# A DiT attention block: V with its features on the partitions, V Wo gated first, and the probabilities applied last

## The chip, the cores and the metric

The kernel runs on one core of one Trainium2 chip. The core has a matrix engine (TensorE, PE in the profile), a vector engine (VectorE, DVE), an activation engine (ScalarE, ACT), a general engine (GpSimd, POOL), and a sequencer that issues transfers (SyncE, SP). The metric is the device time of one execution in microseconds. It was 95.58 us before the change, the median of three runs (95.51 to 95.72). The profile was taken from one further execution, of 95.64 us.

## The reference: what is computed

```python
B, N, D = (2, 256, 1152)
mod = (_silu(c) @ w_mod).reshape(B, 6, 1, D)
shift_a, scale_a, gate_a, shift_m, scale_m, gate_m = [mod[:, i] for i in range(6)]
h = _layernorm(x, axis=-1) * (1 + scale_a) + shift_a
qkv = h @ wqkv
q, k, v = (qkv[..., :D].copy(), qkv[..., D:2 * D].copy(), qkv[..., 2 * D:].copy())
p = _softmax(jnp.einsum('bqd,bkd->bqk', q, k) * D ** (-0.5), axis=-1)
a = jnp.einsum('bqk,bkd->bqd', p, v) @ wo
return x + gate_a * a
```

All inputs and the output are bfloat16. There is one head of 1152 features. The last two lines are what the change regroups: x + gate * ((P V) Wo) can be computed as x + P ((V Wo) * gate), because the gate depends on the batch and the output column and not on the token.

## The kernel before, in words

The 512 tokens are four blocks of 128 (`TT`), two to a batch (`NQ`); the 1152 features are nine blocks of 128 (`KT`) or three chunks of 384 (`CW`, `NCH`). The program order of each engine is the order in the source: the helpers `ten`, `vec`, `sca`, `gps` and `spq` record every instruction, and `pin` at the end fixes that order, so every engine's instructions show the recorder's line, 85, and the profile is read by tile names. PSUM is eight banks, given out in turn by `bank` from a ring, so a sum's bank is taken again eight sums later.

Up to the scores nothing is changed. `hT` is the modulated h with features on the partitions, `qkT` holds q and k in the same way, `s_tiles` are the scores. The softmax (`scores`, `exps`, `probs`) runs on VectorE and ScalarE beside TensorE, and `turn` transposes the probabilities by DMA into `pT_sbs` (keys on the partitions). The gate takes another way: VectorE sums w_mod times silu(c) into `gacc` (`gate_steps`), and GpSimd adds over the partitions with two `partition_all_reduce`, one for each batch, into `gate_bc`, which then holds the gate on every partition. GpSimd starts them only after the last of VectorE's gate steps (`gate_done`).

The part that the change replaces has three stages on TensorE:

- Lines 622 to 628 and 648 (`v_group`): V with the tokens on the partitions, 12 groups (four token blocks by three column chunks) of nine matmuls of 384 columns. ScalarE copies each group to `v_sb`.
- Lines 663 to 672: for each batch, P V transposed, two feature blocks to a bank, 36 matmuls of 256 columns. VectorE and ScalarE copy them in turn to `attnT`.
- Lines 674 to 711: attnT times Wo, block of tokens by block. A sum is multiplied by the gate into `ga` (VectorE), x is added to it (VectorE), and a block is stored by SP when its row is whole. The last block of tokens goes in column chunks of 448, 288, 224 and 192 with stores of their own.

For the last chunk of the last block the gate is multiplied into 192 columns of Wo ahead of time (`wo_last`, by `gated_columns`): eight of nine feature blocks by VectorE between its sums, the ninth by GpSimd behind its second all-reduce. There x enters the sum as one more matmul (identity times x), ScalarE copies the sum out, and the store is issued on ScalarE's own DMA queue.

SP's DMA queue carries all loads, in the order of need (V's weights in three column chunks `chunks_w`, then Wo in three), then the four transposes, then the stores.

Of the kernel before, what the change touches and what calls it, by code (L numbers as in the profile page):

```python
# [8 lines left out]
ALU = mybir.AluOpType  # L9
AX = mybir.AxisListType  # L10
F32 = mybir.dt.float32
BF16 = mybir.dt.bfloat16
# [4 lines left out]
def kernel(  # L17
# [9 lines left out]
    nc = tc.nc  # L27
    P = 128
    B, N, D = x.shape
    T = B * N  # L30
    KT = D // P
    TT = T // P
    NQ = N // P
    CW = 384
    NCH = D // CW
# [10 lines left out]
    out_f = out.rearrange("b n d -> (b n) d")  # L46
# [7 lines left out]
    act = ctx.enter_context(tc.tile_pool(name="act", bufs=1))  # L54
    work = ctx.enter_context(tc.tile_pool(name="work", bufs=2))
    const = ctx.enter_context(tc.tile_pool(name="const", bufs=1))
# [9 lines left out]
    def bank(shape, name, dtype=None, where=None):  # L66
        if where is None:
            where = ring[turn_no[0] % len(ring)]
            turn_no[0] += 1
        return where[0].tile(shape, dtype or F32, tag=where[1], name=name)  # L70
# [21 lines left out]
    vec = _Rec(nc.vector, dve_seq)  # L92
    sca = _Rec(nc.scalar, act_seq)
    ten = _Rec(nc.tensor, pe_seq)
    spq = _Rec(nc.sync, sp_seq)
# [14 lines left out]
    def one(t):  # L110
        return slice(t * P, (t + 1) * P)
# [3 lines left out]
    ident = const.tile([P, P], BF16)  # L115
    gps.memset(ident, 0.0)
    gps.affine_select(
        out=ident, in_=ident, compare_op=ALU.not_equal, fill=1.0, base=0,
# [8 lines left out]
        out=mask, in_=mask, compare_op=ALU.is_ge, fill=0.0, base=0,  # L127
# [3 lines left out]
        out=mask, in_=mask, compare_op=ALU.is_ge, fill=0.0, base=2,  # L131
# [4 lines left out]
    x_sb = act.tile([P, TT, D], BF16)  # L136
# [7 lines left out]
    chunks_w = [wpool.tile([P, KT, CW], BF16, tag=f"wchunk{i}", name="wV") for i in range(NCH)]  # L144
# [121 lines left out]
    hT = act.tile([P, KT, T], BF16)  # L266
# [69 lines left out]
    def evac(on_dve, out_ap, in_ap):  # L336
        if on_dve:
            return vec.tensor_copy(out=out_ap, in_=in_ap)
        return sca.copy(out=out_ap, in_=in_ap)
# [201 lines left out]
    wO = wmpool.tile([P, KT, D], BF16, tag="wH")  # L541
# [31 lines left out]
    for f in range(QACC, KT):  # L573
        ps = bank([P, T], "psQ")
# [6 lines left out]
    for b in range(B):  # L581
        s_ps = bank([P, NQ, N], "s_ps")
        for i in range(NQ):
            tq = b * NQ + i
            for k in range(KT):
                ten.matmul(s_ps[:, i, :], lhsT=qkT[:, k, tq * P : (tq + 1) * P], rhs=qkT[:, KT + k, tok(b)],
                           start=(k == 0), stop=(k == KT - 1))
        s_tiles.append(s_ps)

    nmxs, p_fs, rsums, pns, pT_sbs = {}, {}, {}, {}, []  # L590
# [26 lines left out]
            spq.dma_start_transpose(out=pT[:, :, i * P : (i + 1) * P], in_=pns[b][:, i, :])  # L617
        pT_sbs.append(pT)

    v_sb = act.tile([P, TT, D], BF16, tag="a1")  # L620

    def v_group(gidx):
        t, vc = divmod(gidx, NCH)
        wt = chunks_w[vc]
        ps = bank([P, CW], "ps")
        for k in range(KT):
            ten.matmul(ps, lhsT=hT[:, k, t * P : (t + 1) * P], rhs=wt[:, k, :], start=(k == 0), stop=(k == KT - 1))
        evac(False, v_sb[:, t, vc * CW : (vc + 1) * CW], ps)

    gate_bc = act.tile([P, B, D], F32, tag="gb")  # L630

    gate_steps(11)
# [12 lines left out]
        ar = gps.partition_all_reduce(gate_bc[:, b, :], gacc[:, b, :], P, bass.bass_isa.ReduceOp.add)  # L645
        tc.add_manual_dep(ar.ins, gate_done, SYNC_SCHED, reason="keep gpsimd off the shared port")

    for gidx in range(TT * NCH):
        v_group(gidx)

    attnT = act.tile([P, KT, T], BF16, tag="a2")
    TAIL = (192,)
    TAILW = sum(TAIL)
    wo_last = const.tile([P, KT, TAILW], BF16)

    def gated_columns(eng, k0, k1):
        eng.tensor_tensor(out=wo_last[:, k0:k1, :], in0=wO[:, k0:k1, D - TAILW :],
                          in1=gate_bc[:, B - 1, D - TAILW :].unsqueeze(1).to_broadcast([P, k1 - k0, TAILW]),
                          op=ALU.mult)

    gated_columns(gps, KT - 1, KT)

    for b in range(B):
        for gi, dv0 in enumerate(range(0, KT, 2)):
            ndv = min(2, KT - dv0)
            ps = bank([P, 2, N], "ps")
            for dd in range(ndv):
                dv = dv0 + dd
                for j in range(NQ):
                    ten.matmul(ps[:, dd, :], lhsT=v_sb[:, b * NQ + j, dv * P : (dv + 1) * P],  # L670
                               rhs=pT_sbs[b][:, j, :], start=(j == 0), stop=(j == NQ - 1))
            evac(gi % 2 == 0, attnT[:, dv0 : dv0 + ndv, b * N : (b + 1) * N], ps[:, :ndv, :])

    todo = {4: (0, 3), 6: (3, 6), 8: (6, KT - 1)}
    for t in range(TT):
        b = t // NQ
        o_sb = work.tile([P, D], BF16, tag="o_sb")
        if t < TT - 1:
            chunks = [(oc * CW, CW) for oc in range(NCH)]
            dma_after = {NCH - 1: (0, D)}  # L680
        else:
            chunks, c0 = [], 0
            for w_ in (448, 288, 224) + TAIL:
                chunks.append((c0, w_))
                c0 += w_
            dma_after = {1: (0, chunks[2][0]), 2: (chunks[2][0], D - TAILW), 3: (D - TAILW, D)}
        for ci, (c0, w_) in enumerate(chunks):
            cs = slice(c0, c0 + w_)
            last = (t == TT - 1) and (ci == len(chunks) - 1)
            pregated = (t == TT - 1) and c0 >= D - TAILW  # L690
            ps = bank([P, w_], "ps")
            if pregated:
                ten.matmul(ps, lhsT=ident, rhs=x_sb[:, t, cs], start=True, stop=False)
            for k in range(KT):
                ten.matmul(
                    ps, lhsT=attnT[:, k, t * P : (t + 1) * P],
                    rhs=(wo_last[:, k, c0 - (D - TAILW) : c0 - (D - TAILW) + w_] if pregated else wO[:, k, cs]),
                    start=(k == 0 and not pregated), stop=(k == KT - 1),
                )
            if pregated:  # L700
                sca.copy(out=o_sb[:, cs], in_=ps)
            else:
                ga = work.tile([P, 448], F32, tag="ga")
                vec.tensor_tensor(out=ga[:, :w_], in0=ps, in1=gate_bc[:, b, cs], op=ALU.mult)
                vec.tensor_tensor(out=o_sb[:, cs], in0=ga[:, :w_], in1=x_sb[:, t, cs], op=ALU.add)
                if t * NCH + ci in todo:
                    gated_columns(vec, *todo[t * NCH + ci])
            if ci in dma_after:
                d0, d1 = dma_after[ci]
                dma_eng = nc.scalar if last else spq  # L710
                dma_eng.dma_start(out=out_f[t * P : (t + 1) * P, d0:d1], in_=o_sb[:, d0:d1])

    pin(pe_seq)
    pin(dve_seq)
# [33 lines left out]
```

## Time and profile before

| | us |
|---|---|
| median of three runs | 95.58 |
| the profiled execution | 95.64 |
| its span, first to last instruction | 93.9 |
| TensorE busy | 88.6 |
| VectorE busy | 70.3 |
| ScalarE busy | 34.0 |
| GpSimd busy | 21.2 |
| V, from its first matmul to that of the next stage | 51.76 to 69.31 |
| P V | 69.31 to 73.24 |
| attnT times Wo, its last matmul's end | 73.24 to 91.07 |

The page gives busy times for each engine. A matmul's record is longer than its share of TensorE, since matmuls are pipelined: a group's pace is read from the starts of the stages. A row of a timeline has the start, the length, the engine, the line, the operation, what it writes and reads, its shape and the number of merged instructions; in brackets stands how long the engine was idle before it and what ended that. `ps` are the sums in PSUM, and all three stages above use that name. A row of the chain of waits has the start, the length and the engine with the line. In the list of transfers the last number of a row is the time from issue to landing.

### The profile page before, as it was taken

How to read it: one execution, taken by the hardware profiler on the slowest of the kernel's cores; microseconds unless marked ns; L12 is line 12 of the kernel's file. 1: busy time of each engine (PE TensorE's matmuls, PEld its weight loads, DVE VectorE, ACT ScalarE, POOL GpSimd, SP SyncE). 2: the span in 40 equal slices, each digit the busy share in tenths (PEclk: the TensorE clock that was granted, in tenths of full speed). 3: DMA queues.
4: the chain of work that ended last, by engine and by line, in shares of the span. 5: the costliest groups of instructions: out<-in, count | busy, mean ns of one | idle time of the engine just before them, and what ended most of it. 6: DMA issues, size and time to landing. Idle time of an engine off the chain costs nothing.

```text
span 93.9 us, 1692 instructions
## 1 busy us (share of the span) xinstructions
PE 88.6 (94%) x664; PEld 52.9 (56%) x664; DVE 70.3 (75%) x134; ACT 34.0 (36%) x69; POOL 21.2 (23%) x26
## 2 busy tenths in 40 slices
PE   3989899999999999999999999999999999999980
PEld 1358684545445444444469656565679656655660
DVE  2498689254997988999998899990018587899980
ACT  5189689002553610284320688324246300000010
POOL 5623000810000000000000000008999990003000
PEclk9999999999999999999999999999999999999999
DMA  2999999999999999999999602200000000303123
GB/s 29 334 309 377 380 392 358 377 411 409 405 406 410 409 410 412 399 373 366 383 409 411 269 9 56 61 2 0 0 0 0 0 0 7 126 0 126 57 92 103
DMA packets 17232, 21.31 MB, mean 227 GB/s; under 512 B 2377, under 2 KB 10569, under 8 KB 17225
## 3 DMA queue, kind: packets, MB, share of 16 engines
q1 hardware_dynamic: 16809, 21.15, 62.1%
q8 instruction: 5, 0.08, 0.4%
q10 hardware_dynamic: 416, 0.05, 0.4%
q14 instruction: 2, 0.02, 0.0%
HBM read 19.76 MB, written 1.18 MB: 223 GB/s over the span
## 4 chain that ended last, share of the span: by engine, by line
PE 86%; DMA 6%; SPq 4%; issue 1%; ACT 0%
PE ps L85 42%; PE psQ L85 19%; PE acc L85 10%; PE psK L85 7%; DMA wK<-in_wqkv_dram 6%; PE s_ps L85 4%; SPq L85 4%; PE psE L85 2%; PE psS L85 1%; PE psH L85 1%; PE tp L85 1%; ACT o_sb L85 0%; PE bc_ps L85 0%; PE pT L85 0%
## 5 line engine op out<-in xcount | busy, mean ns | idle before, releaser
L85 POOL PARTITION_ALL_REDUCE gate_bc<-gacc x2 | 13.7, 6886 | 44.6 <-DVE gacc L85 44.6
L85 DVE SCALAR_TENSOR_TENSOR gacc<-wG,scT_f,gacc 128x1152 f32<-128x1152 bf16 x16 | 22.4, 1416 | 0.4
L85 PE MATMUL ps<-wV,hT 128*128 128x384 bf16 x108 | 17.7, 326 | 0.0
L85 PE MATMUL psQ<-hT,wQ 128*128 128x512 bf16 x81 | 17.6, 379 | 0.0
L85 PE MATMUL ps<-wO,attnT 128*128 128x384 bf16 (+3 forms) x108 | 17.0, 319 | 0.0
L85 PEld LDWEIGHTS <-attnT 128*128 128x128 bf16 x117 | 11.3, 98 | 6.3
L85 PEld LDWEIGHTS <-hT 128*128 128x128 bf16 x108 | 10.6, 98 | 6.9
L85 PEld LDWEIGHTS <-wK 128*128 128x128 bf16 x109 | 9.4, 97 | 7.5 <-DMA wK<-in_wqkv_dram 0.7
L85 PEld LDWEIGHTS <-wQ 128*128 128x128 bf16 x81 | 7.9, 98 | 9.5
L85 PE MATMUL acc<-hTs,wK 128*128 128x512 bf16 (+2 forms) x65 | 11.2, 313 | 0.0
L85 ACT CAST qkT<-psQ 128x512 bf16<-128x512 f32 x9 | 4.9, 597 | 10.6 <-PE psQ L85 10.6
L85 DVE CAST attnT<-ps 128x512 bf16<-128x512 f32 (+1 forms) x6 | 3.5, 603 | 6.8 <-PE ps L85 6.8
L85 ACT CAST v_sb<-ps 128x384 bf16<-128x384 f32 x12 | 5.5, 476 | 7.9 <-PE ps L85 7.9
L85 DVE TENSOR_TENSOR ga<-ps,gate_bc 128x384 f32<-128x384 f32 (+3 forms) x12 | 6.4, 537 | 2.3 <-PE ps L85 2.3
L85 PE MATMUL psK<-hTs,wK 128*128 128x512 bf16 x28 | 7.0, 379 | 0.0
L85 DVE TENSOR_TENSOR o_sb<-ga,x_sb 128x384 bf16<-128x384 f32 (+3 forms) x12 | 6.5, 542 | 0.4
L85 ACT CAST o_sb<-ps 128x192 bf16<-128x192 f32 x1 | 0.3, 318 | 17.3 <-PE ps L85 17.3
L85 DVE TENSOR_TENSOR hT<-hTs,held 128x512 bf16<-128x512 bf16 x9 | 5.7, 682 | 0.4 <-ACT held L85 0.4
L85 PE MATMUL junk_ps<-junk 128*128 128x512 bf16 x11 | 4.1, 553 | 1.5 <-DVE junk L85 1.5
L85 DVE BATCH_NORM_STATS2 stats<-x_sb 128x6 f32<-128x384 bf16 x6 | 3.1, 542 | 2.2 <-DMA x_sb<-in_x_dram 2.2
L85 PE MATMUL ps<-pT,v_sb 128*128 128x256 bf16 x36 | 4.1, 272 | 0.0
L85 PE MATMUL s_ps<-qkT 128*128 128x256 bf16 x36 | 4.1, 273 | 0.0
(81 smaller groups left out, 83.2 us busy)
## 6 DMA issues: line engine op xcount, KB each, us to landing
wG<-in_w_mod_dram SPq DMA_DIRECT2D x3, 864.0 KB, 12.5
wV<-in_wqkv_dram SPq DMA_DIRECT2D x3, 864.0 KB, 13.4
wO<-in_wo_dram SPq DMA_DIRECT2D x3, 864.0 KB, 9.1
wH<-in_w_mod_dram SPq DMA_DIRECT2D x2, 1152.0 KB, 9.5
wQ<-in_wqkv_dram SPq DMA_DIRECT2D x4, 576.0 KB, 11.7
wK<-in_wqkv_dram SPq DMA_DIRECT2D x7, 288.0 KB, 7.3
wS<-in_w_mod_dram SPq DMA_DIRECT2D x3, 320.0 KB, 5.9
x_sb<-in_x_dram SPq DMA_DIRECT2D x3, 288.0 KB, 3.2
```

The lines of the kernel that those rows point to most:

```text
L85: r = fn(*a, **k)
```

## The change

V is now computed with its features on the partitions (`vT`): nine groups of nine matmuls of 512 columns, copied by ScalarE. Then u = (V Wo) * gate with the tokens on the partitions (`vo`): VectorE multiplies by the gate as it takes a sum out of PSUM, so u is complete but for P. Then P u (`attend`), two matmuls for each token block and column chunk, with the transposed probabilities as weights; VectorE adds x on the way out into `o_sb`, which is now one tile for all four blocks. `ga` and `attnT` are gone.

The two stages are interleaved by hand, so that P on a chunk comes one or two `vo` groups after the `vo` groups that it reads. The column chunks are 384 wide in batch 0; in batch 1 the last chunk is split into 256 (`CL`) and 128 (`CE`). The last 128 columns use Wo with the gate of batch 1 already in it (`wo_last`, now 128 wide and used for both blocks of batch 1), so ScalarE can copy these sums to u. For the last piece of block 3 x enters by the identity matmul and ScalarE copies and stores, as before; the other pieces end on VectorE and SP. In the last steps the two halves of P u on `CE` are split, so that the first halves of blocks 2 and 3 come ahead of the second halves. There are seven stores where there were six.

```diff
-    for gidx in range(TT * NCH):
-        v_group(gidx)
...
+    vT = act.tile([P, KT, T], BF16, tag="a1")
+    for f in range(KT):
+        wt, i = chunks_w[f // NCH], f % NCH
+        ps = bank([P, T], "psV")
+        for k in range(KT):
+            ten.matmul(ps, lhsT=wt[:, k, i * P : (i + 1) * P], rhs=hT[:, k, :], start=(k == 0), stop=(k == KT - 1))
+        evac(False, vT[:, f, :], ps)
...
+    u_sb = act.tile([P, TT, D], BF16, tag="a2")
+    o_sb = act.tile([P, TT, D], BF16, name="o_sb")
+    wo_last = const.tile([P, KT, P], BF16)
...
     gated_columns(gps, KT - 1, KT)
...
+    def vo(t, c0, w_):
+        cs = slice(c0, c0 + w_)
+        ps = bank([P, w_], "psU")
+        for f in range(KT):
+            ten.matmul(ps, lhsT=vT[:, f, one(t)], rhs=wO[:, f, cs] if w_ > P else wo_last[:, f, :],
+                       start=(f == 0), stop=(f == KT - 1))
+        if w_ > P:
+            vec.tensor_tensor(out=u_sb[:, t, cs], in0=ps, in1=gate_bc[:, t // NQ, cs], op=ALU.mult)
         else:
+            sca.copy(out=u_sb[:, t, cs], in_=ps)
...
+    def attend(t, c0, w_, steps=range(NQ), on_act=False):
+        b, i = divmod(t, NQ)
+        cs = slice(c0, c0 + w_)
+        for j in steps:
+            if j == 0:
+                pso[t] = bank([P, w_], "psO")
+                if on_act:
+                    ten.matmul(pso[t], lhsT=ident, rhs=x_sb[:, t, cs], start=True, stop=False)
+            ten.matmul(pso[t], lhsT=pT_sbs[b][:, j, i * P : (i + 1) * P], rhs=u_sb[:, b * NQ + j, cs],
+                       start=(j == 0 and not on_act), stop=(j == NQ - 1))
+        if NQ - 1 not in steps:
+            return
+        if on_act:
+            sca.copy(out=o_sb[:, t, cs], in_=pso[t])
+        else:
+            vec.tensor_tensor(out=o_sb[:, t, cs], in0=pso[t], in1=x_sb[:, t, cs], op=ALU.add)
+
+    CA, CB, CC = [(i * CW, CW) for i in range(NCH)]
+    CL, CE = (2 * CW, CW - P), (D - P, P)
+    vo(0, *CA)
+    vo(1, *CA)
+    vo(0, *CB)
+    attend(0, *CA)
+    vo(1, *CB)
+    attend(1, *CA)
+    vo(0, *CC)
+    attend(0, *CB)
+    vo(1, *CC)
+    attend(1, *CB)
+    vo(2, *CA)
+    attend(0, *CC)
+    store(0, 0, D)
+    gated_columns(vec, 0, 3)
+    vo(3, *CA)
+    attend(1, *CC)
+    store(1, 0, D)
+    gated_columns(vec, 3, 6)
+    vo(2, *CB)
+    attend(2, *CA)
+    gated_columns(vec, 6, KT - 1)
+    vo(3, *CB)
+    attend(3, *CA)
+    vo(2, *CL)
+    attend(2, *CB)
+    vo(3, *CL)
+    attend(3, *CB)
+    store(3, 0, CL[0])
+    vo(2, *CE)
+    attend(2, *CL)
+    store(2, 0, CE[0])
+    vo(3, *CE)
+    attend(3, *CL)
+    store(3, CL[0], CE[0])
+    attend(2, *CE, steps=range(1))
+    attend(3, *CE, steps=range(1), on_act=True)
+    attend(2, *CE, steps=range(1, NQ))
+    attend(3, *CE, steps=range(1, NQ), on_act=True)
+    store(2, CE[0], D)
+    store(3, CE[0], D, sca)
```

More of the change, by code (lines that the diff above doesn't have):

```diff
@@ L618, in turn @@
         pT_sbs.append(pT)
[L620 to L628, printed above, removed]
     gate_bc = act.tile([P, B, D], F32, tag="gb")
@@ L646 @@
         tc.add_manual_dep(ar.ins, gate_done, SYNC_SCHED, reason="keep gpsimd off the shared port")
-    for gidx in range(TT * NCH):
-        v_group(gidx)
[L651 to L654, printed above, removed]
+    vT = act.tile([P, KT, T], BF16, tag="a1")
[5 more added lines that the diff above has]
+        evac(False, vT[:, f, :], ps)
@@ L656, in gated_columns @@
+    u_sb = act.tile([P, TT, D], BF16, tag="a2")
+    o_sb = act.tile([P, TT, D], BF16, name="o_sb")
+    wo_last = const.tile([P, KT, P], BF16)
     def gated_columns(eng, k0, k1):
-        eng.tensor_tensor(out=wo_last[:, k0:k1, :], in0=wO[:, k0:k1, D - TAILW :],
-                          in1=gate_bc[:, B - 1, D - TAILW :].unsqueeze(1).to_broadcast([P, k1 - k0, TAILW]),
-                          op=ALU.mult)
+        eng.tensor_tensor(out=wo_last[:, k0:k1, :], in0=wO[:, k0:k1, D - P :],
+                          in1=gate_bc[:, B - 1, D - P :].unsqueeze(1).to_broadcast([P, k1 - k0, P]), op=ALU.mult)
@@ L661 @@
     gated_columns(gps, KT - 1, KT)
[L663 to L680, printed above, removed]
-        else:
[L682 to L711, printed above, removed]
@@ new lines, in vo, with store @@
+    def vo(t, c0, w_):
[6 more added lines that the diff above has]
+            vec.tensor_tensor(out=u_sb[:, t, cs], in0=ps, in1=gate_bc[:, t // NQ, cs], op=ALU.mult)
+        else:
+            sca.copy(out=u_sb[:, t, cs], in_=ps)
+    def store(t, c0, c1, eng=spq):
+        eng.dma_start(out=out_f[t * P : (t + 1) * P, c0:c1], in_=o_sb[:, t, c0:c1])
@@ new lines @@
+    pso = {}
+    def attend(t, c0, w_, steps=range(NQ), on_act=False):
[14 more added lines that the diff above has]
+            vec.tensor_tensor(out=o_sb[:, t, cs], in0=pso[t], in1=x_sb[:, t, cs], op=ALU.add)
```

## The prediction

> **What bounds the kernel now.** I read the span and the engine lines first, then the chain of waits, then the timeline of each engine from 50 us to the end. The span:
>
> ```profile
> span 93.9 us, 1692 instructions
> PE 88.6 (94%) x664; PEld 52.9 (56%) x664; DVE 70.3 (75%) x134; ACT 34.0 (36%) x69; POOL 21.2 (23%) x26
> PEclk9999999999999999999999999999999999999999
> ```
>
> TensorE is busy to the end, at full granted clock in every slice. The chain of waits (start, length, what) says whether anything else counts; the early rows price small matmuls:
>
> ```profile
> 1.19 0.06 issue
> ...
> 10.78 0.82 PE acc L85 x10
> ...
> 12.32 0.32 PE acc L85 x5
> ...
> 30.51 17.48 PE psQ L85 x81
> 48.00 3.93 PE s_ps L85 x36
> 51.93 39.15 PE ps L85 x262
> 91.08 0.02 issue
> 91.10 0.32 ACT o_sb L85
> ```
>
> From 30.51 to 91.08 the chain is TensorE alone. So the change is worth what it does to the number and width of matmuls, to waits between them, and to what follows the last one. The starts of the stages, from TensorE's timeline (start, length):
>
> ```profile
> 51.76 17.71 PE L85 MATMUL ps<-wV,hT 128*128 128x384 bf16 x108
> 69.31 4.09 PE L85 MATMUL ps<-pT,v_sb 128*128 128x256 bf16 x36
> 73.24 16.99 PE L85 MATMUL ps<-wO,attnT 128*128 128x384 bf16 x108
> 90.07 0.25 PE L85 MATMUL ps<-x_sb,ident 128*128 128x192 bf16 x1
> 90.16 0.91 PE L85 MATMUL ps<-wo_last,attnT 128*128 128x192 bf16 x9
> ```
>
> 108 V matmuls of 384 columns fill 69.31 - 51.76 = 17.55 us: 0.1625 us each, with no wait. The 36 of 256 columns take 73.24 - 69.31 = 3.93: 0.109 each. 81 of 512 take 17.48 (psQ): 0.216 each. The ten acc pieces at 10.78 are five of 256 and five of 128 columns: (0.82 - 5 x 0.109) / 5 = 0.055 us for 128 columns. The pitch is columns over 2.4 per ns plus 2.5 ns; the 27 matmuls of 448, 288 and 224 columns inside the 73.24 row fit it too.
>
> **The change on TensorE.** V becomes V^T: 81 matmuls of 512 columns in place of 108 of 384: 17.48 for 17.55. V Wo has 90 of 384, 18 of 256 and 18 of 128: 14.63 + 1.97 + 0.99 = 17.59. P on that has 20 of 384, 4 of 256, 4 of 128 and the identity: 3.25 + 0.44 + 0.28 = 3.97. Sum 39.04. Before: 17.55 + 3.93 + (90.07 - 73.24 = 16.83) + ten of 192 columns, 0.083 each = 39.14. So TensorE gains 0.10 us, if it waits nowhere new: the products are regrouped and their columns are all but the same.
>
> **The change beside TensorE.** Rows of VectorE, then of ScalarE:
>
> ```profile
> 50.00 0.69 DVE L85 TENSOR_TENSOR p_f<-s_ps,held 128x512 f32<-128x512 f32 x1 [0.20 <-PE s_ps L85]
> ...
> 74.98 0.56 DVE L85 TENSOR_TENSOR ga<-ps,gate_bc 128x384 f32<-128x384 f32 x1 [1.11 <-PE ps L85]
> ...
> 86.36 0.56 DVE L85 TENSOR_TENSOR o_sb<-ga,x_sb 128x384 bf16<-128x384 f32 x1
> 86.83 0.55 DVE L85 TENSOR_TENSOR ga<-ps,gate_bc 128x384 f32<-128x384 f32 x1
> ...
> 87.89 0.55 DVE L85 TENSOR_TENSOR wo_last<-wO,gate_bc 128x384 bf16<-128x384 bf16 x1
> ...
> 90.04 0.46 DVE L85 TENSOR_TENSOR o_sb<-ga,x_sb 128x288 bf16<-128x288 f32 x1
> 90.42 0.38 DVE L85 TENSOR_TENSOR ga<-ps,gate_bc 128x224 f32<-128x224 f32 x1
> 90.83 0.39 DVE L85 TENSOR_TENSOR o_sb<-ga,x_sb 128x224 bf16<-128x224 f32 x1
> ```
>
> ```profile
> 48.03 0.58 ACT L85 CAST qkT<-psQ 128x512 bf16<-128x512 f32 x1 [1.36 <-PE psQ L85]
> ...
> 69.51 0.48 ACT L85 CAST v_sb<-ps 128x384 bf16<-128x384 f32 x1 [0.98 <-PE ps L85]
> ...
> 91.10 0.32 ACT L85 CAST o_sb<-ps 128x192 bf16<-128x192 f32 x1 [17.29 <-PE ps L85]
> ```
>
> ScalarE: nine casts of 0.58 for twelve of 0.48, one per 1.94 us of matmuls; hidden. The last one starts when V^T ends, at 51.76 + 17.48 = 69.24 plus the 0.17 us of pipeline tail that a record has over its pitch, and is done by 70.02; the ninth matmul of V Wo, its first reader, comes at 69.24 + 8 x 0.1625 = 70.54. Gone are its four casts of attnT, and VectorE's six, which TensorE covered; they gain nothing. Ahead of ScalarE's copies of the 128-column blocks nothing is queued.
>
> VectorE: 12 multiplies and 12 adds become 10 multiplies and 12 adds, and the adds now read PSUM and x instead of ga and x. The multiplies read the same pair as before (0.56). An add from PSUM has no row of this form; the nearest is the multiply from PSUM (0.56), and the add from SBUF costs 0.56 too, so I take 0.56, with 0.69 (the 512-wide one at 50.00) as the far end; that end stays hidden, since work of 0.5 to 0.6 stands every 0.8 us until 89 us. The gated columns are 384, 384 and 256 wide for 576, 576 and 384: 0.55 each at most, in gaps between sums; their cover is the bank ring, eight deep, of which two or three are in use.
>
> GpSimd's block shrinks from 192 to 128 columns. Its rows in its timeline, and the gate's row among the instructions of that tile (ns, first and last start):
>
> ```profile
> 63.72 13.69 POOL L85 PARTITION_ALL_REDUCE gate_bc<-gacc  x2 [44.62 <-DVE gacc L85]
> 84.37 0.87 POOL L85 TENSOR_TENSOR wo_last<-wO,gate_bc 128x192 bf16<-128x192 bf16 x1 [6.96 <-issue]
> ```
>
> ```profile
> L85 POOL PARTITION_ALL_REDUCE gate_bc<-gacc x2: 6851/6886/6921, 63.7 to 70.5; - x2
> ```
>
> By the record the first gate is there at 63.72 + 6.85 = 70.57, the second at 77.41. The gate is now wanted sooner: the first V Wo sum is readable at 69.24 + 1.46 + 0.17 = 70.87 (before, at 74.9), batch 1's at 80.95. So by the record nothing waits. GpSimd's block, done at 85.2, is read at about 89.5; hidden by 4 us.
>
> **The new handoffs.** Each P step reads u blocks that have just been evacuated. The delay from an engine's end to TensorE's start, from one place where it did wait (VectorE's timeline, then the loads', then TensorE's):
>
> ```profile
> 10.69 0.65 DVE L85 TENSOR_SCALAR xc<-x_sb,nmean 128x512 bf16<-128x512 bf16 x2
> ```
>
> ```profile
> 11.38 0.27 PEld L85 LDWEIGHTS <-xc 128*128 128x128 bf16 x4
> ```
>
> ```profile
> 11.44 0.39 PE L85 MATMUL tp<-ident,xc 128*128 128x128 bf16 x4
> ```
>
> From 11.34 to 11.38 and 11.44: 0.04 to 0.10. From TensorE's record end to the evacuation it is 0.03 (91.07 to 91.10). With pitches added up from 69.24, P(0) of the first chunk starts at 73.63; its second u block is done at 72.34 + 0.17 + 0.56 = about 73.0. The same slack, 0.5 to 0.8, holds for the others down to the end, where pieces get short. V Wo of block 3's 256 columns ends its pitch at 88.77; VectorE multiplies from 88.96 for 0.42 (between the 224 and 288 rows), 89.38, and with the handoff 89.45; TensorE wants it at 89.59: 0.14 left. V Wo of block 3's last 128 columns ends at 90.30; ScalarE copies from 90.49 for 0.27 (0.32 less 64 columns at 0.82 ns, the slope of the 192 and 384 rows), 90.76, with the handoff 90.80 to 90.86; TensorE is ready at 90.30 + 0.22 + 3 x 0.055 = 90.68. A wait of 0.12 to 0.18; I take 0.15. TensorE's last record then ends near 91.10, for 91.07 before.
>
> **The tail.** The last issues and the page's landing times:
>
> ```profile
> 91.25 0.33 SPq L85 DMA_DIRECT2D out_dram<-o_sb  x1
> 91.45 0.36 ACTq L711 DMA_DIRECT2D out_dram<-o_sb  x1
> ```
>
> ```profile
> out_dram<-o_sb SPq DMA_DIRECT2D x3, 288.0 KB, 2.1
> ...
> out_dram<-o_sb SPq DMA_DIRECT2D x1, 184.0 KB, 1.8
> ...
> out_dram<-o_sb SPq DMA_DIRECT2D x1, 56.0 KB, 1.6
> ...
> out_dram<-o_sb ACTq DMA_DIRECT2D x1, 48.0 KB, 1.6
> ```
>
> Before, the last store is issued on ScalarE's queue at 91.45 and lands at 93.05. After, that chain is 91.10 + 0.03 + 0.27 + 0.03 = 91.43. But SP has two small stores behind one another: P of block 3's 256 columns is readable at 90.30 + 0.22 + 0.17 = 90.69, VectorE adds from 90.72 for 0.42, SP issues at 91.17 for 0.33 to 0.36, and with the gap of 0.05 to 0.06 between SP's issues (1.19 in the chain) the store of block 2's last columns is issued at 91.57. Its data are there at about 91.4 (sum 91.05, add 0.28 by the same slope), so SP's turn ends last, not the data. With 1.6 us to landing, the nearest row for 32 KB, that is 93.17: 0.12 later. Extending the landing rows downwards would give 1.55, and 0.07; I keep 1.6.
>
> **The sum.** TensorE -0.10, the wait for ScalarE's copy +0.15 (absorbed by SP's chain), SP's second small store 0.12 behind the old last issue: **+0.12 us**. The profiled execution took 95.64, its span 93.9 and 1.74 around it; it would be 95.76. That execution is 0.06 over the median of 95.58, against which the forecast is **95.70**. A difference under 0.2% (0.19 us) is about what a measurement of this kernel can't tell from none.
>
> **Rivals.** (1) The gate is late. The first reader before, at 74.98, came no sooner than its sum; that bounds the first gate to between 70.57 and 74.95. Two multiplies and the handoff take 1.2 us, so P(0) at 73.63 waits if the gate comes after 72.4, and by 2.5 us if at 74.95: 95.8 to 98.2. For it: the page calls GpSimd's spans rough, and 6.96 us behind the sums are unexplained. Against: the second sum starts as the first ends. [...] Chance 0.09.
>
> (2) Small matmuls cost more. At 12.32 five of 128 columns took 0.32, 0.064 each. The point from which it counts is 0.06; at 0.08 the 23 pieces cost 0.57 more, part of it taking the place of the 0.15 wait: 96.1 to 96.3. Against it is the 0.055 of the ten acc pieces. [...] Chance 0.07.
>
> (3) Handoffs are slower than 0.10, or adds from PSUM longer. From 0.14 on, P on the 256 columns waits as well; with 0.25 more at each of the last handoffs the end moves 0.3 to 0.6: 96.0 to 96.3. For it: few handoffs are measured. Chance 0.14.
>
> (4) The tail gets shorter. If 32 KB land in 1.3 us, or SP's issues are quicker, the -0.10 shows and the copy is 0.05 shorter: 95.35 to 95.5. For it: landing falls with size. Against: 56 and 48 KB land alike. Chance 0.14.
>
> **Numbers.** The forecast has 0.56; its own range is 95.5 to 95.95, from the landing, the handoff and the add; 0.40 of it is within 0.2%, 0.12 slower, 0.04 faster. Rival 4 gives 0.10 faster and 0.04 same, rivals 1 to 3 give 0.30 slower. So faster 0.14, same 0.44, slower 0.42. The range 95.35 to 96.6 leaves out the late part of rival 1 and the low end of rival 4.
>
> **What would show it.** V^T filling 17.5 us with no wait; V Wo starting near 69.25; VectorE's first multiply at about 71, with TensorE as its releaser and not GpSimd; 0.1 to 0.2 us without matmuls after the last V Wo group; SP's last issue near 91.57, after ScalarE's. The prediction is wrong if TensorE has gaps between 70 and 77 (gate), if the 128-column groups take more than 0.55 us per nine, or if the last store is ScalarE's.

## The result and the profile after

The changed kernel took 96.09 us (median of 22 runs, 95.64 to 96.46), the kernel before 95.71 (median of 22 runs beside it). The ratio is 1.0034, with a 95% interval of 1.0018 to 1.0051: about 0.33 us slower (0.17 to 0.49), where +0.12 was forecast; the time lies inside the forecast's range of 95.35 to 96.6. The profiled execution took 95.89 us with a span of 94.0, where the one before took 95.64 with 93.9.

The two executions do not start alike: they reach the same point, the first matmul of the scores, 0.10 us apart. All comparisons of places in two traces below count from that matmul. Here it is in TensorE's timeline of the kernel before (start, length, and so on as above):

```profile
47.83 4.09 PE L85 MATMUL s_ps<-qkT 128*128 128x256 bf16 x36
```

And TensorE's timeline of the changed kernel, from that point to the end:

```profile
47.73 4.09 PE L85 MATMUL s_ps<-qkT 128*128 128x256 bf16 x36
51.88 17.43 PE L85 MATMUL psV<-hT,wV 128*128 128x512 bf16 x79
```

```profile
69.14 4.55 PE L85 MATMUL psU<-wO,vT 128*128 128x384 bf16 x27
73.53 0.49 PE L85 MATMUL psO<-u_sb,pT 128*128 128x384 bf16 x2
...
88.98 0.67 PE L85 MATMUL psU<-wo_last,vT 128*128 128x128 bf16 x9
89.48 0.38 PE L85 MATMUL psO<-u_sb,pT 128*128 128x256 bf16 x2
89.70 0.67 PE L85 MATMUL psU<-wo_last,vT 128*128 128x128 bf16 x9
90.20 0.44 PE L85 MATMUL psO<-u_sb,pT 128*128 128x256 bf16 x3
90.48 0.22 PE L85 MATMUL psO<-x_sb,ident 128*128 128x128 bf16 x1
90.53 0.46 PE L85 MATMUL psO<-u_sb,pT 128*128 128x128 bf16 x3
```

(Two records of V^T are missing; the stage begins at 47.73 + 3.93 = 51.66.) TensorE has no gap from there to 90.58. V^T takes 17.48 us, V Wo and P follow each other without a wait, nine matmuls of 128 columns take 89.48 - 88.98 = 0.50. The last record ends at 90.99, 43.26 us behind the scores' first matmul, for 91.07, 43.24 behind it, before. So the regrouping on TensorE comes out even, as forecast. A narrower stretch shows the one wait, before the last two matmuls:

```profile
90.72 0.27 PE L85 MATMUL psO<-u_sb,pT 128*128 128x128 bf16 x2
```

Then the ends of VectorE, ScalarE and SP, one fence for each timeline:

```profile
70.88 0.56 DVE L85 TENSOR_TENSOR u_sb<-psU,gate_bc 128x384 bf16<-128x384 f32 x1 [7.48 <-PE psU L85]
72.27 0.56 DVE L85 TENSOR_TENSOR u_sb<-psU,gate_bc 128x384 bf16<-128x384 f32 x1 [0.83 <-PE psU L85]
...
89.90 0.42 DVE L85 TENSOR_TENSOR o_sb<-psO,x_sb 128x256 bf16<-128x256 f32 x1 [0.16 <-PE psO L85]
90.62 0.64 DVE L85 TENSOR_TENSOR o_sb<-psO,x_sb 128x256 bf16<-128x256 f32 x2 [0.30 <-PE psO L85]
```

```profile
90.41 0.27 ACT L85 CAST u_sb<-psU 128x128 bf16<-128x128 f32 x1 [0.45 <-PE psU L85]
91.03 0.27 ACT L85 CAST o_sb<-psO 128x128 bf16<-128x128 f32 x1 [0.36 <-PE psO L85]
91.33 0.36 ACTq L85 DMA_DIRECT2D out_dram<-o_sb  x1
```

```profile
91.08 0.33 SPq L85 DMA_DIRECT2D out_dram<-o_sb  x1
```

```profile
91.50 0.41 SPq L85 DMA_DIRECT2D out_dram<-o_sb  x1
```

VectorE's first multiply (70.88) waits for its sum and not for the gate. ScalarE's copy of block 3's u ends at 90.68, and the matmul that needs it starts at 90.72. On ScalarE's queue the last store is issued about as early as before (43.60 us behind the scores' first matmul for 43.62). On SP's queue the store of block 2's last 128 columns has its data at 91.26, VectorE's last add; it is issued at 91.50, behind the store of block 3's 256 columns (91.08), and its issue takes 0.41 us where the one ahead of it takes 0.33. SP is now the last engine to issue: its issue ends at 91.91, 44.18 us behind the scores' first matmul. Before, the last issue was ScalarE's, ending at 91.81, 43.98 behind it. So the last issue ends 0.20 us later, in the place that the prediction named.

The end of an issue is not yet the end of the span. The traces also hold, finer than the views print it, when each store has landed and what SP does last. The last store lands 45.17 us behind the scores' first matmul before (it is ScalarE's) and 45.29 after (it is SP's). That is 0.12 us later. SP then closes the program with a row of waits, one behind the other in a fixed order, each for the semaphores of transfers, the counters that a landing raises. Before, one such wait comes behind the last landing; after, it is three, 0.06 us apart. From the last landing to the end of the span it takes 0.87 us before and 1.00 after, 0.13 more. The span ends 46.04 us behind the mark before and 46.29 after, 0.25 later in all.

The rest lies outside the span. The time of a run less its span is 1.87 us on average for the changed kernel (22 runs) and 1.76 for the kernel before (29 runs, beside the first experiments below). That is 0.11 us more. 0.25 + 0.11 = 0.36, close to the 0.33 measured and inside its interval.

### The profile page after: what moved, and what is told of

It reads as the page before. It is cut to its first block, busy times and chain, and to the rows that moved or that the text cites. A ratio compares the mean times of both kernels' runs of the same rounds, so it can differ in the third digit from the quotient of the medians.

```text
span 94.0 us, 1621 instructions
## 1 busy us (share of the span) xinstructions
PE 88.8 (94%) x632; PEld 49.7 (53%) x638; DVE 65.4 (70%) x129; ACT 31.7 (34%) x64; POOL 20.4 (22%) x26
## 4 chain that ended last, share of the span: by engine, by line
PE 94%; DVE 1%; issue 1%; ACT 0%
PE psU L85 19%; PE psQ L85 19%; PE psV L85 18%; PE acc L85 10%; PE psK L85 6%; PE junk_ps L85 5%; PE psO L85 4%; PE s_ps L85 4%; PE tp L85 2%; PE psE L85 2%; PE psS L85 2%; PE psH L85 1%; DVE xc L85 1%; DVE junk L85 1%; ACT o_sb L85 0%
## 5 line engine op out<-in xcount | busy, mean ns | idle before, releaser
L85 PE MATMUL psU<-wO,vT 128*128 128x384 bf16 (+1 forms) x108 | 18.2, 317 | 0.0
L85 PE MATMUL psV<-hT,wV 128*128 128x512 bf16 x79 | 17.4, 379 | 0.1
L85 DVE TENSOR_TENSOR u_sb<-psU,gate_bc 128x384 bf16<-128x384 f32 (+1 forms) x12 | 6.4, 536 | 14.0 <-PE psU L85 14.0
L85 PEld LDWEIGHTS <-vT 128*128 128x128 bf16 x126 | 11.7, 98 | 6.5
L85 PEld LDWEIGHTS <-wV 128*128 128x128 bf16 x81 | 7.9, 98 | 9.3
L85 ACT CAST vT<-psV 128x512 bf16<-128x512 f32 x9 | 5.1, 583 | 8.3 <-PE psV L85 8.1
L85 DVE TENSOR_TENSOR o_sb<-psO,x_sb 128x384 bf16<-128x384 f32 (+2 forms) x13 | 6.5, 509 | 0.5 <-PE psO L85 0.5
L85 PE MATMUL junk_ps<-junk 128*128 128x512 bf16 x11 | 4.9, 631 | 1.5 <-DVE junk L85 1.5
L85 PE MATMUL psO<-u_sb,pT 128*128 128x384 bf16 (+2 forms) x28 | 6.1, 303 | 0.0
L85 PEld LDWEIGHTS <-junk 128*128 128x128 bf16 (+1 forms) x13 | 1.7, 136 | 4.9 <-issue 3.3
```

What stands on the lines that cost most here:

```text
L85: r = fn(*a, **k)
```

## The experiments

Three theories were set against each other. A: SP's second small store sets the end. B: TensorE's waits for the last copies set it. C: the loss lies before V or outside the span. A fourth, D, came up on the way.

**The yardstick.** The changed kernel again, in two series with the experiments.

> The changed kernel unaltered, beside the others. Theory A (SP's second small store sets the end): the forecast term of +0.12 us, with up to 0.1 more for the length of that issue: ratio to the kernel before 1.001 to 1.003. Theory B (TensorE's waits for the last copies set the end) and theory C (the loss lies before V, or outside the span) expect the same ratio, since they only place it elsewhere: in the trace A wants the last issue on SP at about 39.85 us behind the first matmul of V^T's stage, with ScalarE's 0.15 or more ahead of it; C wants V^T to start later.

> The changed kernel unaltered once more, as the yardstick for the three beside it on this chip: ratio 1.003 to 1.005, the last issue 43.8 us behind the first matmul of the scores, which is the first point that both kernels share.

Ratios 1.0047 (1.0021 to 1.0073) and 1.0033 (1.0014 to 1.0052). In both traces the last issue is SP's again and ends 44.18 us behind the scores' first matmul, so the 0.20 us comes back to 0.01. The last landing (45.28) and the end of the span (46.28) come back too, and the time outside the span was 1.87 both times. Over the runs of both series the span is 0.28 us longer on average than that of the kernel before (0.15 to 0.42). The tail gives 0.25 of that, so nothing speaks for a loss before V.

**The last two stores of block 3 merged.**

```diff
     attend(3, *CL)
-    store(3, CL[0], CE[0])
...
-    store(3, CE[0], D, sca)
+    store(3, CL[0], D, sca)
```

> Block 3's last two stores become one of 384 columns on ScalarE's queue, so that SP's last store (block 2's last 128 columns) is issued as soon as its data are there. Theory A: SP's last issue moves from 91.50 to about 91.29, ScalarE's stays at 91.33, which is then the last; 96 KB land in 1.6 to 1.7 us instead of 32 KB in 1.5: the end comes 0.05 to 0.2 us earlier than the changed kernel's, ratio 0.9995 to 1.001. Theory B: no change in TensorE, so the time of the changed kernel, ratio about 1.003. Theory C: the same as B.

> The merged last store a second time, to narrow its interval (1.0012, 0.9987 to 1.0037, the first time). Theory A: 0.2 to 0.35 us below the changed kernel, ratio 0.9995 to 1.002. Theory B: ratio of the changed kernel.

Ratios 1.0012 (0.9987 to 1.0037) and 1.0019 (0.9998 to 1.0039); on the same chips the changed kernel's median was 0.28 and 0.16 us higher. SP's and ScalarE's last issues in the first of the two traces:

```profile
91.56 0.33 SPq L85 DMA_DIRECT2D out_dram<-o_sb  x1
91.59 0.37 ACTq L85 DMA_DIRECT2D out_dram<-o_sb  x1
```

The scores began at 48.00 there. So SP's store is issued 0.21 us earlier on that clock (43.56 for 43.77), takes 0.33 instead of 0.41, and the last issue ends at 43.96, where the kernel before has 43.98. In the second trace it ends at 43.96 too. But the last landing hardly moves: it is now ScalarE's larger store, at 45.28 in both traces, 0.01 earlier. What falls is the stretch behind it, to 0.84 us, as no closing wait comes behind the last landing, and the time outside the span, to 1.75 and 1.74. TensorE was not touched, so B falls. C keeps what lies outside the span: it goes with the stores here, and not with V.

**The cost by itself in the kernel before.** SP's last store is cut in two.

```diff
+                cuts = [d0, D - TAILW - P, d1] if d1 == D - TAILW else [d0, d1]
+                for e0, e1 in zip(cuts, cuts[1:]):
+                    dma_eng.dma_start(out=out_f[t * P : (t + 1) * P, e0:e1], in_=o_sb[:, e0:e1])
-                dma_eng.dma_start(out=out_f[t * P : (t + 1) * P, d0:d1], in_=o_sb[:, d0:d1])
```

> The suspected cost by itself in the kernel before: SP's last store (columns 736 to 960 of block 3) is issued as two, of 96 and 128 columns, one behind the other, so that SP's last issue comes at about 91.64 instead of 91.25, behind ScalarE's at 91.45. Theory A: 0.15 to 0.25 us slower than the kernel before, ratio 1.0015 to 1.0025. Theory B and C: ratio 1.000.

> The split last store of the kernel before a second time (1.0019, 0.9994 to 1.0044, the first time). Theory A: ratio 1.002 to 1.003. Theory B: 1.000.

Ratios 1.0019 (0.9994 to 1.0044) and 1.0025 (1.0003 to 1.0046). The trace of the first:

```profile
91.16 0.81 SPq L85 DMA_DIRECT2D out_dram<-o_sb  x2
91.34 0.36 ACTq L713 DMA_DIRECT2D out_dram<-o_sb  x1
```

Two issues behind one another take 0.81 us, and the last ends at 91.97, 44.25 behind the scores' first matmul (47.72): 0.27 later than uncut, with nothing else changed. The last store, SP's, lands at 45.41 in this trace and at 45.40 in the other, 0.24 and 0.23 later than uncut: this is the kind of cost that the forecast's term stands for, by itself. Each interval alone touches or nearly touches 1; both agree with A in size.

**TensorE's wait taken away.** Block 3's last V Wo group moves ahead of block 2's P step.

```diff
     vo(2, *CE)
+    vo(3, *CE)
     attend(2, *CL)
     store(2, 0, CE[0])
-    vo(3, *CE)
     attend(3, *CL)
```

> The changed kernel with block 3's last V Wo group moved ahead of block 2's P step on the 256 columns, so that TensorE has work while ScalarE copies: its wait of 0.13 us before the last two matmuls goes and its last record ends 0.13 us earlier; ScalarE's store is issued 0.13 us earlier. The two adds of the 256 columns come closer together on VectorE (the second at 90.73 to 91.15 instead of 90.62 to 91.04), so SP's last issue comes at 91.57 to 91.61 instead of 91.50. Theory A: 0 to 0.1 us slower than the changed kernel. Theory B: 0.13 us faster.

The ratio is 1.0073 (1.0046 to 1.01): slower still. VectorE's, ScalarE's and SP's ends in its trace, where the scores began at 47.74:

```profile
90.42 0.95 DVE L85 TENSOR_TENSOR o_sb<-psO,x_sb 128x256 bf16<-128x256 f32 x3 [0.66 <-PE psO L85]
```

```profile
90.91 0.27 ACT L85 CAST o_sb<-psO 128x128 bf16<-128x128 f32 x1 [0.45 <-PE psO L85]
```

```profile
90.87 1.31 SPq L85 DMA_DIRECT2D out_dram<-o_sb  x3
```

ScalarE's last copy starts at 90.91, 0.13 earlier than in the changed kernel, so TensorE's wait is gone as expected. But VectorE's three adds now come in one piece, and SP issues three stores without a pause, of which the last ends at 92.18 (44.44, for 44.18); its store lands 0.36 later than the changed kernel's last one. TensorE ended earlier and the kernel was slower: B is out. The size was missed. I had counted the second and third store of that row only, at 0.0 to 0.1 us, and not the 256 KB one ahead of them, which now crowds them.

The ends side by side, in us. The first two columns count from the scores' first matmul, the third has SP's closing waits behind the last landing, the fourth the averages of the series. The last two compare with the kernel before: the sum of what the span's end and the time outside add, and what the ratios give.

| | last landing | span's end | waits | outside | sum | measured |
|---|---|---|---|---|---|---|
| before | 45.17 | 46.04 | 1 | 1.76, 1.75 | | |
| changed, three traces | 45.28 to 45.29 | 46.28 to 46.29 | 3 | 1.87 | 0.36 | 0.33, 0.45, 0.32 |
| merged, two traces | 45.28 | 46.11 to 46.12 | 0 | 1.75, 1.74 | 0.06 | 0.11, 0.18 |
| cut in the kernel before, two traces | 45.41, 45.40 | 46.34 | 2 | 1.71, 1.72 | 0.25, 0.27 | 0.18, 0.24 |
| V Wo group first | 45.64 | 46.64 | 3 | 1.86 | 0.71 | 0.70 |

From the last landing to the end of the span it is 0.84 us with no wait behind it, 0.87 with one, 0.93 to 0.94 with two and 1.00 with three. No run changes the order of these waits alone, so their price is read from the traces and not tested by itself. So A is right in part: a second small store at SP's end lands last in the changed kernel and costs 0.12 us there, and the rest of the 0.36 is 0.13 in SP's closing waits and 0.11 outside the span.

**The gate made late.** GpSimd sums batch 1's gate first.

```diff
-    for b in range(B):
+    for b in (1, 0):
         ar = gps.partition_all_reduce(gate_bc[:, b, :], gacc[:, b, :], P, bass.bass_isa.ReduceOp.add)
```

> GpSimd sums batch 1's gate first and batch 0's second, so that batch 0's gate is there at 77.3 instead of 70.46 us. It tells how much cover the gate has in the changed kernel, and whether GpSimd's record says when it is there. By the record VectorE's first multiply starts at about 77.3 with GpSimd as its releaser, the first P step comes at 78.4 instead of 73.5, and the whole end shifts: 4.9 us slower, ratio 1.051. If the sum's result were there later than its record, more than that by the same amount; if TensorE had other work to do meanwhile, less.

> The same swap in the kernel before, whose first multiply by the gate is at 74.98: VectorE starts 2.4 us late, TensorE goes on into the other PSUM banks, VectorE has 1.2 us of idle time to make up for it before 81 us and none after, so its last add ends about 1.2 us late: 0.8 to 1.4 us slower, ratio 1.008 to 1.015. If the gate were not needed so early, ratio 1.000.

The changed kernel became 1.0703 (1.0665 to 1.0742), the kernel before 1.0036 (1.0016 to 1.0056). In the changed kernel VectorE's and TensorE's timelines and the sums by stretch (us, busy of each engine, granted clock, share of the DMA engines) read:

```profile
77.60 1.49 DVE L85 TENSOR_TENSOR u_sb<-psU,gate_bc 128x384 bf16<-128x384 f32 x3 [13.95 <-POOL gate_bc L85]
```

```profile
69.39 4.55 PE L85 MATMUL psU<-wO,vT 128*128 128x384 bf16 x27
78.21 0.94 PE L85 MATMUL psO<-u_sb,pT 128*128 128x384 bf16 x2 [4.26 <-DVE u_sb L85]
78.95 3.01 PE L85 MATMUL psU<-wO,vT 128*128 128x384 bf16 x9
81.80 0.49 PE L85 MATMUL psO<-u_sb,pT 128*128 128x384 bf16 x2
```

```profile
74.00:78.00 4.00, 0.00 (x0) 0.00 (x0) 0.40 (x1) 0.00 (x0) 3.56 (x1) 1.00 0.00 0
78.00:80.00 2.00, 1.71 (x6) 0.73 (x6) 1.64 (x4) 0.00 (x0) 0.00 (x0) 0.59 0.00 0
80.00:82.00 2.00, 2.00 (x9) 0.93 (x8) 0.00 (x1) 0.00 (x0) 0.00 (x0) 0.56 0.00 0
82.00:84.00 2.00, 2.00 (x14) 1.23 (x13) 1.24 (x3) 0.00 (x0) 0.00 (x0) 1.00 0.00 0
```

GpSimd's second sum ends by its record at 63.87 + 13.69 = 77.56 in that execution, and VectorE starts at 77.60 with GpSimd as its releaser: here the record tells when the gate is there. The first P step comes 78.21 - 69.39 = 8.82 us after V Wo's start instead of 73.53 - 69.14 = 4.39: 4.43 us later, near the forecast. On top comes what I had left out: after 4.26 us without matmuls the granted clock reads 0.59 and 0.56, and the next nine matmuls take 3.01 us for 1.63. In steps of half a microsecond the trace has 0.50 all the way from 78.50 to 81.50; the rows above mix this with full clock at their edges. By the next P step (81.80, 12.41 after V Wo's start, for 75.32 - 69.14 = 6.18) the loss is 6.23. So in this run 4.26 us without matmuls stand ahead of a little over 3 us at a clock of 0.50; why the clock fell and what brought it back was not shown. In the kernel before TensorE went on, and VectorE made up for more than I had granted it, since its adds and multiplies then ran back to back (a pair every 1.07 us, for 1.46 without the swap): 0.36% of 95.52 us is 0.34 us for the 1.2 expected. The same delay of the gate costs the changed kernel some twenty times what it cost before.

**The special tail taken out.**

```diff
-    gated_columns(gps, KT - 1, KT)
...
-    gated_columns(vec, 0, 3)
...
-    vo(2, *CL)
+    vo(2, *CC)
     attend(2, *CB)
-    vo(3, *CL)
+    vo(3, *CC)
     attend(3, *CB)
-    store(3, 0, CL[0])
...
+    store(3, 0, CC[0])
+    attend(2, *CC)
+    store(2, 0, D)
+    attend(3, *CC)
+    store(3, CC[0], D, sca)
```

> The changed kernel without its special tail: batch 1's last 384 columns go like batch 0's, multiplied by the gate on VectorE, with no gated Wo columns and no identity matmul; the last store of block 3 is issued by ScalarE after VectorE's add, block 2's whole row by SP. By the durations of the changed kernel's trace TensorE waits about 0.45 us for the last multiply (0.56 plus 0.24 of pipeline tail and handoffs, less one P step of 0.33), its last record ends 0.2 later, and the last issue comes near 91.99 instead of 91.50; 288 KB issued at 91.5 land 2.1 later. Theory A and B: 0.5 to 0.7 us slower than the changed kernel, ratio 1.008 to 1.011. Theory C: nearer to the changed kernel than that.

The ratio is 1.1022 (1.0981 to 1.1062), 9.8 us slower: no theory had that. GpSimd's timeline at the start of the execution, first of the kernel before and then of this one:

```profile
0.79 0.20 POOL L85 MEMSET ident<- 128x128 bf16 x1 [0.29 <-POOLq L732]
1.28 0.29 POOL L85 TENSOR_SCALAR_AFFINE_SELECT ident<-ident 128x128 bf16<-128x128 bf16 x1 [0.29 <-POOL ident L85]
```

```profile
0.78 0.20 POOL L85 MEMSET ident<- 128x128 bf16 x1 [0.30 <-POOLq L741]
10.58 0.28 POOL L85 TENSOR_SCALAR_AFFINE_SELECT ident<-ident 128x128 bf16<-128x128 bf16 x1 [9.59 <-issue]
```

The loss is at the other end of the program. GpSimd sits 9.59 us, for nothing that the profile shows, before its first `affine_select`, and the identity, the ones row and silu(c) behind it hold up TensorE. What differs for GpSimd is only that its last work is now the two sums. Theory D: the sums leave GpSimd a wait ahead of its next work of another kind, the multiply behind them takes that wait (the idle 6.96 us before it), and without it the next execution pays at its start. What the wait is for is the author's guess (the next expectation has code brought back), and no row shows it. Two runs test the rest.

```diff
+    tiny = const.tile([P, 2], F32, name="tiny")
+    gps.tensor_tensor(out=tiny, in0=gate_bc[:, B - 1, 0:2], in1=gate_bc[:, B - 1, 0:2], op=ALU.mult)
```

> The kernel without the special tail, plus one tiny multiply of two columns by GpSimd behind its two sums (its result is not used). In the run without it GpSimd's first shifted fill at the start of the kernel sat 9.6 us idle and everything behind it came later. Theory D (the standard GpSimd operation behind the sums brings its code back, and without it the next execution pays for that at its start): the 9 us go, GpSimd shows about 7 us of idle before the tiny multiply, and what is left is the worth of the special tail, 0.5 to 0.7 us over the changed kernel: ratio 1.008 to 1.011. Rival (the plain tail or the missing block itself costs the 9 us): ratio stays near 1.10.

and, in the kernel before, the ninth block given to VectorE:

```diff
-    gated_columns(gps, KT - 1, KT)
...
-    todo = {4: (0, 3), 6: (3, 6), 8: (6, KT - 1)}
+    todo = {4: (0, 3), 6: (3, 6), 8: (6, KT)}
```

> The kernel before with GpSimd's block of Wo given to VectorE, as a ninth in its last piece, so that GpSimd's last work is its two sums. Theory D: 9 to 10 us slower (ratio 1.095 to 1.105), all of it ahead of 15 us in the trace, where GpSimd waits about 9 us before its first shifted fill. Rival: only VectorE's longer piece shows, 0.15 us in a stretch where it has no idle time, so 0 to 0.3 us slower.

With the tiny multiply the plain tail fell to 1.0067 (1.0045 to 1.0089); without its block the kernel before rose to 1.1104 (1.1055 to 1.1154). GpSimd's rows, of the one at its end and of the other at its start:

```profile
84.21 0.18 POOL L85 TENSOR_TENSOR tiny<-gate_bc 128x2 f32<-128x2 f32 x1 [7.00 <-issue]
```

```profile
10.48 0.28 POOL L85 TENSOR_SCALAR_AFFINE_SELECT ident<-ident 128x128 bf16<-128x128 bf16 x1 [9.49 <-issue]
```

Both ways round, a multiply behind the sums decides over 9 to 10 us at the start: without it the scores' first matmul comes at 56.90 and 58.16 us, for 47.73 and 47.83 in the kernels that have one. The idle times are 6.81 to 7.42 us behind the sums and 9.49 and 9.59 at the start. That one execution inherits what the last one left is inferred from these runs; what GpSimd does in that time, no row names.

With that out of the way, the special tail is worth the difference between 1.0067 and the changed kernel's 1.0033 to 1.0047, 0.2 to 0.3 us, for the 0.5 to 0.7 expected; the intervals overlap, so the times alone don't fix it. By the traces the span ends 0.55 us later than the changed kernel's (46.84 behind the scores' first matmul for 46.29), near the forecast, and the time outside it is 0.13 shorter (1.74 for 1.87). TensorE waited 0.32 us there and not 0.45, since it got three matmuls in ahead of the wait, and VectorE's adds ran closer together.

## Why the prediction was right, and where its sizes were off

**TensorE's work** (-0.10 us): held. V Wo starts 69.14 - 47.73 = 21.41 us after the scores' first matmul, for 69.31 - 47.83 = 21.48 at the end of V before. All pitches held: 81 matmuls of 512 columns filled 17.48 us (0.216 each), 27 of 384 filled 73.53 - 69.14 = 4.39 (0.1625 each), two of 256 filled 89.70 - 89.48 = 0.22 (0.11 each), and the 0.055 for 128 columns held too (0.50 for nine). Rival 2 is out: no run shows its 0.08 for 128 columns, and the two groups of nine here ran at 0.055.

**The wait for ScalarE's copy** (0.15): measured 0.13. Block 3's first half, the matmul behind the identity's, starts at 90.53 and has its 0.055 us of pitch; the next one starts at 90.72 and not at 90.585. The handoff was 0.04 (90.68 to 90.72), the lower end of the bounds; rival 3 is out. That this wait cost nothing beside SP's queue was part of the sum. The run without it fits: TensorE's last record ended 0.12 us earlier, and the end still followed SP's last store. It is no clean test, since the same edit crowded SP's stores. One sum on the way has a slip: 72.34 holds the 0.17 already, so the second u block was due at 72.90, and the slack is 0.7 us. It was done at 72.83 in the changed kernel's trace, 0.70 ahead of its reader, so nothing hangs on it.

**The gate**: VectorE's first multiply started 0.11 us after its sum, not after GpSimd. Rival 1 is out. The swap shows that its mechanism is real: with a gate later than the rival had it, TensorE waits, and the lower clock behind so long a wait (0.50 behind 4.26 us) comes on top, which the rival's price did not have.

**The tail** (+0.12): held, by its own mark, the last landing (45.29 for 45.17). The last issue starts 43.77 us behind the scores' first matmul, where the prediction had 91.57 - 47.83 = 43.74. Its store landed 1.52 us behind that, for the 1.6 taken, and ScalarE's before landed in 1.56, for 1.6. So the forecast had both landings 0.05 us late, and that they cancel is luck. The issue that took 0.41 us for 0.33 to 0.36 is inside that landing time. What the sum left out is the stretch from the last landing to the end of the span, 0.13 us longer. The end of an issue would be a worse mark: from there to the end of the span it is 2.07 to 2.36 us over all traces here, from the last landing 0.83 to 1.01.

**What lay around the span** was taken to stay at 1.74. It grew by 0.11 us. It is a property of the program: 1.87 in all three series of the changed kernel, 1.86 in the gate swap and in the run with the V Wo group first, which have the same seven stores; 1.71 to 1.76 in the kernel before, in the kernel before with its store cut (which also has seven), and with the merged store. The plain tail has 1.80, and 1.74 with the tiny multiply. Why is not settled.

**Rival 4** (a shorter tail) is out: 32 KB did land in 1.52 us for 1.6, but not in 1.3, and SP's store landed last.

The forecast of no measurable change had the chance 0.44, slower 0.42; the measured 0.34% lies in the second. The likeliest case named the mechanism, and two terms that it left at zero, 0.13 between the last landing and the span's end and 0.11 outside the span, took it over the line.

## What to carry to other kernels

Where a regrouping leaves the matmul columns the same, look at the last three stores: count them by queue, and give a queue one small store at the end, not two (cutting one in two cost the kernel before 0.18 and 0.24 us in two series). Count to the last landing, and then add what SP still waits through behind it (0.84 to 1.00 us here). A gate, or any other late operand, that moves from the last stage to the middle one takes its cover with it: find how late it may come before you move its reader. And before a little operation is taken from behind other work of its engine, as GpSimd's multiply was here, look at what the next execution's start would pay (9 to 10 us here).

## What the runs showed of the hardware that was not expected

- GpSimd's wait at its start went with what it runs last. The two kernels whose last GpSimd work is `partition_all_reduce` have 9.59 and 9.49 us of idle time before the first `affine_select`; a two-column multiply behind the sums leaves 7.00 us at the end instead, where nothing waits. That one execution leaves this to the next is inferred, and what it is was not shown.
- SP's closing waits count: 0.84 us from the last landing to the end of the span with none behind it, 1.00 with three.
- A store issued on SP directly behind another takes 0.39 to 0.42 us (the changed kernel, the cut store, the V Wo group first) where one that follows a pause takes 0.33.
- After 4.26 us without matmuls TensorE ran at a granted clock of 0.50 from 78.50 to 81.50 us, which with the edges added 1.8 us to the wait itself.
- The time outside the profiled span differs by 0.1 to 0.15 us between kernels that differ in their stores; within one kernel the averages of a series agree to 0.03 us (1.76, 1.75 and 1.73 in the kernel before, 1.87 three times in the changed one).
